# Head features split by parity, weights loaded as whole row pairs, and a reordered prologue in a fused attention and gated-unit kernel

## The chip, the cores and the metric

The kernel runs on one core of a Trainium2 chip. The time is the device time of one execution in microseconds, as the median of several executions; it is 1.6 to 1.9 us above the span, which is the time from the first to the last instruction in the profiled execution. Shorter is better. Every run is marked fast or slow by its clock and its distance from the fastest run of the same kernel. All ratios here are the mean time of one kernel's fast runs over the mean of the other's fast runs of the same rounds, so they are not quite the ratio of the medians that stand beside them. The bracket behind a ratio is its 95% interval. Slower and faster mean below that this interval excludes 1.

## The reference

The first half is causal attention over 8 batches, 12 heads, 448 positions and 64 features per head. The second half takes the heads side by side as 768 features and applies a causal convolution of five taps, a sigmoid gate, and two 768x768 products.

```python
scores = q @ k.T / sqrt(64);  causal mask;  attn = softmax(scores);  x = attn @ v   # (8, 12, 448, 64)
x = x.transpose(0, 2, 1, 3).reshape(8, 448, 768)
gate = sigmoid(sum(conv_w[t] * shift(x, 4 - t) for t in range(5)))
out = (gate * (x @ w_val)) @ w_out
```

## The kernel before

The work is cut into 24 units of four heads of one batch. A unit goes through `scores` in two stages (TensorE into the four banks of `sc_ps`), exponentials on ScalarE, causal masks on GpSimd, `attend` (the denominators into `den_ps`, the values into `av_ps`), `normalize` on VectorE, which writes the tile `x`, then `conv` and the gate. Three units make a batch; `val` multiplies a batch's x by `w_val` and VectorE multiplies in the gate; `project` multiplies a pair of batches by `w_out`. In the timelines each engine works through its instructions in the order in which the program gives them (in the trace before, a gate product whose last matmul ended at 60.85 us began only at 65.00, behind the transposes of unit 8 that the program has ahead of it and that waited for their loads), and the whole schedule is set by hand.

The 64 features of a head are stored as two halves of 32. In partition 32*h+d of the tile `x` stand feature d of head h and, in a second column block, feature 32+d. That is why a weight load is made of many small pieces: feature d and feature 32+d are 32 rows apart in DRAM.

```python
def load_wv(i, j):                          # 12 requests in all
    g, swap = VERSIONS[i]
    nc.gpsimd.dma_start(out=wv_sb[i][32 * j:32 * (j + 1)],
                        in_=w_val.rearrange("(g h e d) f -> g h d e f", h=G, e=2, d=32)[g, j ^ swap])
...
def val(b, g, o):
    for e in range(2):
        ...  # six matmuls into o[e]
        nc.vector.scalar_tensor_tensor(     # gate product, one instruction of 128 partitions
            out=gv[g][:, e, S * (b % 2):S * (b % 2 + 1)], in0=gates[NG * b + g][:, e], scalar=1.0,
            in1=o[e][:, 0:S], op0=ALU.add, op1=ALU.mult)
```

The body of the kernel goes two units at a time. The loads of q and k run some units ahead, v runs three units ahead, and `transposes(n + 1)` puts q and k of the next unit into the form that `scores` needs. `keep_clock` issues matmuls of zeros, fillers, that only keep TensorE busy.

```python
def first_half(n):
    exps(n, 0)                              # scores, exponentials and masks of stage 0
    transposes(n + 1)
    cast_v(n)
    load_v(n + 3)
    for m in {4: (6,), 5: (7,), 6: (8, 9), 7: (10, 11)}.get(n, (n + 4,)):
        load_qk(m)
...
exps(3, 1)                                  # the end of the prologue
cast_v(3)
load_v(6)
transposes(4)
next_val((z_ps, den_ps))
```

The softmax here doesn't subtract the row's maximum and nothing guards it: scores larger than these inputs give would overflow.

## Time and profile before

| what | before |
|---|---|
| time, median of 3 runs | 229.48 us (229.06 to 229.81) |
| profiled span | 227.8 us |
| TensorE busy | 209.1 us, 92% |

Two rows of the page's slices are useful to add: each digit is a fortieth of the span, here 5.7 us, in tenths of busy time (PE) or of the full TensorE clock (PEclk).

```profile
PE   7887789889749999999999999999999999989993
PEclk9999999999979999999999999999999999999999
```

From the thirteenth slice on TensorE is nearly full until the end. Almost all that a schedule can win is in the first twelve, and the lowest digit there, a 4, is the hole near 63 us.

### The profile page before, as it was taken

What the parts mean: (1) busy time and instruction counts of PE and PEld (TensorE: products, weight loads), DVE (VectorE), ACT (ScalarE), POOL (GpSimd) and SP (SyncE); (2) the same over time, 40 slices, a digit from 0 to 9 for tenths busy, and PEclk for the clock granted to TensorE, in tenths of its full rate; (3) what the DMA queues carried; (4) which work ended last, traced back from release to release, by engine and by line L of the source; (5) the groups of instructions that cost most, each with busy time, mean ns of one, the idle gap of its engine ahead of it and who ended that gap; (6) DMA issues with size and microseconds to landing.
All of it is one profiled execution on the core that took longest, in us unless ns stands there. A gap on an engine that the chain in (4) does not pass through costs nothing.

```text
span 227.8 us, 8749 instructions
## 1 busy us (share of the span) xinstructions
PE 209.1 (92%) x3822; PEld 114.2 (50%) x3822; DVE 139.6 (61%) x251; ACT 140.0 (61%) x178; POOL 111.5 (49%) x192
## 2 busy tenths in 40 slices
PE   7887789889749999999999999999999999989993
PEld 3334434445325555455555555555655555546551
DVE  7745877565576871868847947939738656270300
ACT  2388226878435779656777687587877777505142
POOL 7189963874950771855727707727535245100000
PEclk9999999999979999999999999999999999999999
DMA  5999999899999289594892993886855120301334
GB/s 85 181 214 201 210 216 202 163 236 210 205 242 202 52 157 308 125 225 82 162 244 82 230 278 73 159 242 114 167 187 154 43 101 3 138 3 72 140 123 156
DMA packets 57696, 36.37 MB, mean 160 GB/s; under 512 B 46133, under 2 KB 54069, under 8 KB 57658
## 3 DMA queue, kind: packets, MB, share of 16 engines
q1 hardware_dynamic: 48922, 22.44, 36.9%
q0 software_dynamic: 8736, 13.37, 34.2%
q8 instruction: 30, 0.49, 0.9%
q14 instruction: 8, 0.07, 0.1%
HBM read 37.76 MB, written 11.01 MB: 214 GB/s over the span
## 4 chain that ended last, share of the span: by engine, by line
PE 70%; DMA 10%; DVE 6%; SPq 5%; ACT 4%; issue 3%; POOL 1%; DVEq 0%; POOLq 0%; ACTq 0%
PE z_ps L263 11%; PE den_ps L263 11%; PE z_ps L285 10%; PE sc_ps L181 8%; PE av_ps L215 6%; PE sc_ps L241 6%; PE den_ps L285 5%; DMA kb<-in_k_dram 5%; PE den_ps L215 4%; SPq L78 3%; PE av_ps L285 3%; ACT pt L190 3%; DMA vf<-in_v_dram 3%; PE sc_ps L285 2%; DMA wv<-wv 2%
## 5 line engine op out<-in xcount | busy, mean ns | idle before, releaser
L190 ACT ACTIVATE pt<-sc_ps 128x1024 bf16<-128x1024 f32 x96 | 93.0, 1022 | 36.6 <-PE sc_ps L181 35.1
L194 POOL TENSOR_SCALAR_AFFINE_SELECT pt<-pt 128x512 bf16<-128x512 bf16 x24 | 15.7, 653 | 71.3 <-ACT pt L190 71.2
L285 PEld LDWEIGHTS <-gv 128*32 128x32 bf16 (+1 forms) x624 | 31.6, 97 | 21.9 <-issue 4.3
L263 PEld LDWEIGHTS <-wv 128*128 128x128 bf16 x288 | 26.4, 98 | 27.1 <-issue 4.3
L181 PE MATMUL sc_ps<-qt,kt 32*128 32x448 bf16 (+3 forms) x768 | 34.9, 280 | 3.3 <-ACT pt L190 1.7
L285 PE MATMUL z_ps<-wo,gv 128*32 128x384 bf16 (+1 forms) x462 | 33.2, 326 | 0.8 <-DVE gv L266 0.8
L200 POOL TENSOR_SCALAR_AFFINE_SELECT pt<-pt 128x512 bf16<-128x512 bf16 x48 | 30.3, 661 | 7.0 <-ACT pt L190 7.0
L181 PEld LDWEIGHTS <-kt 32*128 32x128 bf16 x768 | 18.3, 94 | 29.0 <-issue 17.8
L263 PE MATMUL den_ps<-x,wv 128*128 128x448 bf16 x138 | 30.5, 354 | 1.1 <-DVE x L228 0.8
L263 PE MATMUL z_ps<-x,wv 128*128 128x448 bf16 x138 | 30.2, 353 | 0.9 <-DVE x L228 0.9
L248 ACT ACTIVATE gate<-sc_ps 128x896 f32<-128x896 f32 x23 | 19.9, 914 | 17.9 <-PE sc_ps L241 17.9
L266 DVE SCALAR_TENSOR_TENSOR gv<-gate,den_ps 128x448 bf16<-128x448 f32 x23 | 14.1, 611 | 25.2 <-PE den_ps L263 25.2
L228 DVE TENSOR_TENSOR x<-av_ps,rb 128x448 bf16<-128x448 f32 x48 | 27.7, 620 | 2.6
L215 PE MATMUL av_ps<-pt,vb 128*32 128x448 bf16 (+3 forms) x768 | 26.0, 279 | 1.4 <-DVE vb L86 1.4
L165 DVE STREAM_TRANSPOSE qt<-qb 128x448 uint32<-128x448 uint32 x24 | 22.8, 951 | 7.3 <-DMA qb<-in_q_dram 6.7
L222 DVE STREAM_TRANSPOSE dt<-den_ps 128x448 f32<-128x448 f32 x24 | 15.4, 644 | 18.1 <-PE den_ps L215 18.1
L165 DVE STREAM_TRANSPOSE kt<-kb 128x448 uint32<-128x448 uint32 x24 | 22.3, 931 | 4.4 <-DMA kb<-in_k_dram 4.4
L290 ACT ACTIVATE ob<-z_ps 128x384 f32<-128x384 f32 x29 | 14.3, 493 | 16.2 <-PE z_ps L285 16.2
L86 POOL CAST vb<-vf 128x1024 bf16<-128x1024 f32 x21 | 21.8, 1038 | 0.0
L215 PEld LDWEIGHTS <-vb 128*32 128x32 bf16 x768 | 16.7, 99 | 7.3 <-DVE vb L86 1.6
L266 DVE SCALAR_TENSOR_TENSOR gv<-gate,z_ps 128x448 bf16<-128x448 f32 x23 | 14.1, 614 | 7.9 <-PE z_ps L263 7.9
L215 PE MATMUL den_ps<-pt,ones 128*32 128x448 bf16 (+3 forms) x384 | 15.5, 281 | 3.3 <-DVE gv L266 3.1
(46 smaller groups left out, 177.0 us busy)
## 6 DMA issues: line engine op xcount, KB each, us to landing
out_dram<-ob SPq DMA_DIRECT2D x27, 384.0 KB, 3.9
vf<-in_v_dram SPq DMA_DIRECT2D x72, 128.0 KB, 5.5
qb<-in_q_dram POOLq DMA_DIRECT2D x24, 224.0 KB, 4.7
kb<-in_k_dram POOLq DMA_DIRECT2D x24, 224.0 KB, 5.8
vf<-in_v_dram SPq DMA_DIRECT2D x24, 64.0 KB, 5.5
wv<-in_moe_w_val_dram POOLq DMA_DIRECT2D x12, 96.0 KB, 4.5
wo<-in_moe_w_out_dram POOLq DMA_DIRECT2D x6, 192.0 KB, 8.8
wv<-wv SPq DMA_DIRECT2D x4, 96.0 KB, 5.2
```

Of the source, the lines that this page charges most:

```text
L86: engine.tensor_copy(out=t, in_=vfs.pop(n))
L165: nc.vector.transpose(out=t.bitcast(U32).rearrange("p (b s) -> p s b", s=T), in_=qks.pop((name, n)).rearrange("p s d -> p (s d)").bitcast( ...
L181: nc.tensor.matmul(out=sc_ps[h // 2][:, h % 2, c0:c0 + nq], lhsT=kt[r, e, k0:k0 + 128], rhs=qt[r, e, q0:S], start=e == 0, stop=e == 1, ski ...
L190: nc.scalar.activation(out=pt[:, 2 * hp:2 * hp + 2, 512 * stage:512 * (stage + 1)], in_=sc_ps[hp], func=AF.Exp, scale=D ** -0.5)
L194: nc.gpsimd.affine_select(out=pt[:, :, 0:128], in_=pt[:, :, 0:128], compare_op=ALU.is_ge, fill=0.0, base=0, pattern=[[0, G], [1, 128]], ch ...
L200: nc.gpsimd.affine_select(out=pt[:, :, c:c + 128], in_=pt[:, :, c:c + 128], compare_op=ALU.is_ge, fill=0.0, base=0, pattern=[[0, G], [1, 1 ...
L215: nc.tensor.matmul(out=o, lhsT=w, rhs=pt[:, h, col:col + nq], start=i == 0, stop=i == 3, skip_group_check=True, tile_position=(0, 32 * i_out))
L228: nc.vector.tensor_tensor(out=x[:, dh, 4:S + 4], in0=av_ps[dh][:, 0:S], in1=r, op=ALU.mult)
L248: nc.scalar.activation(out=gates[n], in_=sc_ps[u][:, :, 0:S], func=AF.Tanh, scale=0.5)
L263: nc.tensor.matmul(out=o[e][:, 0:S], lhsT=wv_sb[version(NG * b + cg)][:, ce, f:f + 128], rhs=xs[(NG * b + cg) % 8][:, ce, 4:S + 4], start= ...
L266: nc.vector.scalar_tensor_tensor(out=gv[g][:, e, S * (b % 2):S * (b % 2 + 1)], in0=gates[NG * b + g][:, e], scalar=1.0, in1=o[e][:, 0:S], ...
L285: nc.tensor.matmul(out=o[w * j:w * (j + 1), 0:384], lhsT=gvs[p][g][:, dh, 128 * m + w * j:128 * m + w * (j + 1)], rhs=wo_sb[c][:, f], star ...
```

## The change

The intent is threefold. First, a head's features are split by parity: even features in one column block, odd ones in the other. Rows 2p and 2p+1 of a weight are neighbours in DRAM, so a group's weights load as whole pairs of rows, in nine requests instead of 18. Columns of v and of `w_val` are then taken with a step of two. Second, with this split the gate of an odd feature comes out of the convolution two heads away from the value that it multiplies, so the odd gate product becomes two instructions of 64 partitions. Third, the prologue is reordered: the fillers between the score stages go, units 0 and 1 are attended earlier, v of unit 1 is cast earlier and v of unit 2 on ScalarE, v of units 3 and 4 is held back by a one-word memset on the loading tile, attend(3) and two projections are moved ahead of unit 4, and the loads of q and k for units 6 to 8 are called one unit earlier. The diff, cut to its core:

```diff
-    def load_wv(i, j):
+    def load_wv(i):
         g, swap = VERSIONS[i]
+        src = w_val.rearrange("(g p e) f -> g p e f", g=NG, e=2)[g]
+        if swap:
+            for j in range(G):
+                nc.gpsimd.dma_start(out=wv_sb[i][32 * j:32 * (j + 1)], in_=src[32 * (j ^ 1):32 * ((j ^ 1) + 1)])
+        else:
+            nc.gpsimd.dma_start(out=wv_sb[i], in_=src)
 ...   (load_wo and the convolution weights likewise; wo_sb becomes three tiles)
-                    w = ones[:, int(ci == 1)] if dh == 2 else vb[:, c, h, 32 * dh:32 * (dh + 1)]
+                    w = ones[:, int(ci == 1)] if dh == 2 else vb[:, c, h, dh:D:2]
 ...
-                        j = 2 * ((i ^ swapped(n)) % 2) + dh
+                        j = i ^ swapped(n) ^ (2 * dh)
 ...   (val: columns f + e:f + 256:2 of w_val; the last `late` of six matmuls may come after the other bank's)
+                    for r, at in ((slice(0, 64), slice(64, 128)), (slice(64, 128), slice(0, 64))) if e else ((slice(0, 128),) * 2,):
+                        nc.vector.scalar_tensor_tensor(
+                            out=gv[g][r, e, S * (b % 2):S * (b % 2 + 1)], in0=gates[NG * b + g][at, e], scalar=1.0,
+                            in1=o[e][r, 0:S], op0=ALU.add, op1=ALU.mult)
 ...
-            for m in {4: (6,), 5: (7,), 6: (8, 9), 7: (10, 11)}.get(n, (n + 4,)):
+            for m in {4: (7,), 5: (8,), 6: (9,), 7: (10, 11)}.get(n, (n + 4,)):
 ...
+    def hold_v(n, engine):
+        engine.memset(v_f[n % V_BUFS][:, 0, 0, 0:1], 0.0)
+        load_v(n)
 ...   (prologue, from the second stage of unit 0 on; three keep_clock(3) are gone)
+    exps(1, 0, 2)
+    load_wv(1)
+    load_wv(2)
+    transposes(2)
+    cast_v(0, nc.vector)
+    cast_v(1, nc.vector)
+    exps(1, 1, 2)
+    load_wv(0)
+    values(0)
+    exps(2, 0, 2)
+    exps(2, 1, 2)
+    cast_v(2, nc.scalar)
+    values(1)
+    hold_v(3, nc.vector)
+    values(2)
+    load_qk(3)
+    for g in range(NG):
+        load_wo(g)
+    load_qk(4)
+    hold_v(4, nc.gpsimd)
+    load_v(5)
 ...   (conv(0,1), val, transposes(3), conv(2), val, exps(3, 0), load_qk(5), val)
+    cast_v(3)
+    exps(3, 1)
+    load_qk(6)
+    load_v(6)
+    next_outs(1, (z_ps,))
+    values(3)
+    transposes(4)
+    next_outs(1, (z_ps,))
```

More of the change, by code (lines that the diff above doesn't have):

```diff
@@ L85, in cast_v @@
         t = v_pool.tile([128, 4, G, D], BF16, name="vb")
-        engine.tensor_copy(out=t, in_=vfs.pop(n))
+        if engine is nc.scalar:
+            nc.scalar.activation(out=t, in_=vfs.pop(n), func=AF.Copy)
+        else:
+            engine.tensor_copy(out=t, in_=vfs.pop(n))
         vbs[n] = t
     wv_sb = [sb.tile([128, 2, DM], BF16, name=f"wv{i}") for i in range(len(VERSIONS))]
-    wo_sb = [sb.tile([128, DM], BF16, name=f"wo{i}") for i in range(NE)]
-    def load_wv(i, j):
+    wo_sb = [sb.tile([128, 2, DM], BF16, name=f"wo{g}") for g in range(NG)]
+    def load_wv(i):
         g, swap = VERSIONS[i]
-        nc.gpsimd.dma_start(out=wv_sb[i][32 * j:32 * (j + 1)],
-                            in_=w_val.rearrange("(g h e d) f -> g h d e f", h=G, e=2, d=32)[g, j ^ swap])
+        src = w_val.rearrange("(g p e) f -> g p e f", g=NG, e=2)[g]
+        if swap:
+            for j in range(G):
+                nc.gpsimd.dma_start(out=wv_sb[i][32 * j:32 * (j + 1)], in_=src[32 * (j ^ 1):32 * ((j ^ 1) + 1)])
+        else:
+            nc.gpsimd.dma_start(out=wv_sb[i], in_=src)
     def swap_wv():
@@ L99, in swap_wv, with load_wo @@
             nc.sync.dma_start(out=wv_sb[3][32 * j:32 * (j + 1)], in_=wv_sb[2][32 * (j ^ 1):32 * ((j ^ 1) + 1)])
-    def load_wo(c):
-        nc.gpsimd.dma_start(out=wo_sb[c], in_=w_out[128 * c:128 * (c + 1)])
+    def load_wo(g):
+        nc.gpsimd.dma_start(out=wo_sb[g], in_=w_out.rearrange("(g p e) f -> g p e f", g=NG, e=2)[g])
     NV = 2 * len(VERSIONS)
@@ L138, in conv_weights @@
             for dh in range(2):
-                src = cwn.rearrange("t (g h e d) -> t g h e d", h=G, e=2, d=32)[:, g, :, dh]
+                src = cwn.rearrange("t (g h d e) -> t g h d e", h=G, e=2, d=32)[:, g, :, :, dh]
                 dst = cwp[:, 2 * i + dh].rearrange("t (h d) -> t h d", d=32)
@@ L192, in softmax_numerators @@
                 in_=sc_ps[hp], func=AF.Exp, scale=D ** -0.5)
-        if stage == 0:
-            nc.gpsimd.affine_select(out=pt[:, :, 0:128], in_=pt[:, :, 0:128], compare_op=ALU.is_ge, fill=0.0,
-                                    base=0, pattern=[[0, G], [1, 128]], channel_multiplier=-1)
-            nc.gpsimd.affine_select(out=pt[:, :, 448:512], in_=pt[:, :, 448:512], compare_op=ALU.is_ge, fill=0.0,
-                                    base=64, pattern=[[0, G], [1, 64]], channel_multiplier=-1)
-        else:
-            for c in (512, 832):
-                nc.gpsimd.affine_select(out=pt[:, :, c:c + 128], in_=pt[:, :, c:c + 128], compare_op=ALU.is_ge,
-                                        fill=0.0, base=0, pattern=[[0, G], [1, 128]], channel_multiplier=-1)
+        for c, base, w in ((0, 0, 128), (448, 64, 64)) if stage == 0 else ((512, 0, 128), (832, 0, 128)):
+            nc.gpsimd.affine_select(out=pt[:, :, c:c + w], in_=pt[:, :, c:c + w], compare_op=ALU.is_ge, fill=0.0,
+                                    base=base, pattern=[[0, G], [1, w]], channel_multiplier=-1)
     def attend(n):
@@ L238, in conv @@
                     for u, n in enumerate(units):
-                        j = 2 * ((i ^ swapped(n)) % 2) + dh
+                        j = i ^ swapped(n) ^ (2 * dh)
                         r = slice(32 * i, 32 * (i + 1))
                         nc.tensor.matmul(
-                            out=banks[u][i // 2][32 * j:32 * (j + 1), 0:S], lhsT=cwd[r, 2 * version(n) + dh, t],
+                            out=banks[u][dh][32 * j:32 * (j + 1), 0:S], lhsT=cwd[r, 2 * version(n) + dh, t],
                             rhs=xs[n % 8][r, dh, t:t + S], start=t == 0, stop=t == KW - 1, skip_group_check=True,
@@ L253, with val @@
     sc_banks = [[t[:, i] for i in range(2)] for t in sc_ps]
-    def val(b, g, o):
+    def val(b, g, o, late=0):
         gv = gvs.setdefault(b // 2, [None] * NG)
@@ L258, in val @@
             gv[g] = gv_pool.tile([128, 2, 2 * S], BF16, name=f"gv{g}")
-        for e in range(2):
-            f = 128 * (2 * g + e)
-            for c in range(NE):
-                cg, ce = divmod(c, 2)
-                nc.tensor.matmul(out=o[e][:, 0:S], lhsT=wv_sb[version(NG * b + cg)][:, ce, f:f + 128],
-                                 rhs=xs[(NG * b + cg) % 8][:, ce, 4:S + 4],
-                                 start=c == 0, stop=c == NE - 1, skip_group_check=True)
-            nc.vector.scalar_tensor_tensor(
-                out=gv[g][:, e, S * (b % 2):S * (b % 2 + 1)], in0=gates[NG * b + g][:, e], scalar=1.0,
-                in1=o[e][:, 0:S], op0=ALU.add, op1=ALU.mult)
+        for cs in (range(NE - late), range(NE - late, NE)):
+            for e in range(2):
+                f = 2 * G * 32 * g
+                for c in cs:
+                    cg, ce = divmod(c, 2)
+                    w = wv_sb[version(NG * b + cg)][:, ce, f + e:f + 256:2]
+                    nc.tensor.matmul(out=o[e][:, 0:S], lhsT=w,
+                                     rhs=xs[(NG * b + cg) % 8][:, ce, 4:S + 4],
+                                     start=c == 0, stop=c == NE - 1, skip_group_check=True)
+                if NE - 1 in cs:
+                    for r, at in ((slice(0, 64), slice(64, 128)), (slice(64, 128), slice(0, 64))) if e else ((slice(0, 128),) * 2,):
+                        nc.vector.scalar_tensor_tensor(
+                            out=gv[g][r, e, S * (b % 2):S * (b % 2 + 1)], in0=gates[NG * b + g][at, e], scalar=1.0,
+                            in1=o[e][r, 0:S], op0=ALU.add, op1=ALU.mult)
     vals = [(b, g) for b in range(B) for g in range(NG)]
@@ L285, in project @@
                 nc.tensor.matmul(out=o[w * j:w * (j + 1), 0:384], lhsT=gvs[p][g][:, dh, 128 * m + w * j:128 * m + w * (j + 1)],
-                                 rhs=wo_sb[c][:, f], start=c == 0, stop=c == NE - 1, skip_group_check=True,
+                                 rhs=wo_sb[g][:, dh, f], start=c == 0, stop=c == NE - 1, skip_group_check=True,
                                  **(dict(tile_position=(0, w * j)) if tiles > 1 else {}))
@@ L297, in project, with next_val @@
             nc.sync.dma_start(out=rows, in_=ob)
-    def next_val(banks):
+    def next_val(banks, late=0):
         if vals:
-            val(*vals.pop(0), banks)
+            val(*vals.pop(0), banks, late)
     def next_outs(count, banks, tiles=1):
@@ L332, in second_half @@
             exps(n, 1)
-    wv_pieces = [(i, j) for i in range(NG) for j in range(G)]
-    def load_wvs(count):
-        for _ in range(count):
-            load_wv(*wv_pieces.pop(0))
+    def hold_v(n, engine):
+        engine.memset(v_f[n % V_BUFS][:, 0, 0, 0:1], 0.0)
+        load_v(n)
     load_qk(0)
@@ L355 @@
     exps(0, 1, 2)
-    keep_clock(3)
-    load_wvs(8)
     exps(1, 0, 2)
-    keep_clock(3)
+    load_wv(1)
+    load_wv(2)
     transposes(2)
     cast_v(0, nc.vector)
-    load_v(3)
+    cast_v(1, nc.vector)
     exps(1, 1, 2)
-    keep_clock(3)
-    load_wvs(4)
+    load_wv(0)
[6 more added lines that the diff above has]
+    values(2)
     load_qk(3)
-    exps(2, 0, 2)
-    values(0)
-    exps(2, 1, 2)
+    for g in range(NG):
+        load_wo(g)
     load_qk(4)
-    for c in range(NE):
-        load_wo(c)
-    load_qk(5)
-    cast_v(1, nc.vector)
-    load_v(4)
-    values(1)
-    cast_v(2, nc.vector)
+    hold_v(4, nc.gpsimd)
     load_v(5)
     conv((0, 1), sc_banks)
-    values(2)
+    next_val((z_ps, den_ps), 2)
     transposes(3)
+    conv((2,), [av_ps])
     next_val((z_ps, den_ps))
     exps(3, 0)
+    load_qk(5)
     next_val((z_ps, den_ps))
-    conv((2,), [av_ps])
+    cast_v(3)
     exps(3, 1)
-    cast_v(3)
+    load_qk(6)
     load_v(6)
+    next_outs(1, (z_ps,))
+    values(3)
     transposes(4)
-    next_val((z_ps, den_ps))
-    plan = {2: (2, 0, 1, 0, 1), 3: (2, 0, 0, 0, 0), 4: (0, 1, 2, 1, 2), 5: (2, 0, 0, 0, 0)}
+    next_outs(1, (z_ps,))
+    plan = {2: (1, 1, 1, 0, 1), 3: (2, 0, 0, 0, 0), 4: (0, 1, 2, 1, 2), 5: (2, 0, 0, 0, 0)}
     vals_in = {2: (), 3: (2, 4), 4: (0,), 5: (2, 4)}
@@ L407 @@
         second_half(n)
-        values(n - 1)
+        if p > 2:
+            values(n - 1)
         gap(1, (z_ps,), 4)
```

## The prediction

> **What bounds the kernel now.** I read the page first (busy shares, slices), then busy time by stretch, then the chain of work that ended last, then the timeline of the first 72 us and of the end. The busy shares and the stretches (columns: stretch, its length, then busy us and instruction counts of PE, PEld, DVE, ACT, POOL, then clock, DMA share, GB/s):
>
> ```profile
> PE 209.1 (92%) x3822; PEld 114.2 (50%) x3822; DVE 139.6 (61%) x251; ACT 140.0 (61%) x178; POOL 111.5 (49%) x192
> ```
> ```profile
> 20.00:30.00 10.00, 6.80 (x208) 3.93 (x197) 8.59 (x17) 3.87 (x5) 10.00 (x18) 1.00 1.16 216
> ...
> 60.00:70.00 10.00, 6.71 (x154) 3.60 (x154) 6.01 (x10) 2.70 (x4) 5.91 (x11) 0.83 1.12 221
> ...
> 100.00:150.00 50.00, 49.88 (x1004) 27.82 (x1006) 35.59 (x59) 36.19 (x46) 25.58 (x43) 1.00 0.76 166
> 150.00:200.00 50.00, 49.87 (x1016) 28.16 (x1012) 30.82 (x53) 35.11 (x45) 21.39 (x34) 1.00 0.44 123
> ```
>
> From 100 to 200 us TensorE is idle 0.25 us in all: nothing but fewer or shorter matmuls can help there. The losses are ahead of it: over 0 to 70 us the seven ten-microsecond stretches sum to 57.2 us of PE, so 12.8 us idle, and of the busy time 9.2 us are the 22 filler matmuls[...]. In those 70 us the DMA share is near or above 1 except around 42 to 48. The costliest hole is at 62.5 to 65.7, in the chain view (start, length, what):
>
> ```profile
> 57.20 0.54 POOL qb L67
> 57.74 6.43 DMA kb<-in_k_dram
> 64.18 0.02 issue
> 64.20 0.04 DVE kt L165
> 64.24 0.76 issue
> 65.00 0.61 DVE gv L266
> 65.66 1.05 PE den_ps L215 x12
> ```
>
> The k tile of unit 8 (a unit is four heads of one batch) was requested at 57.7 and took 6.4 us. VectorE works in order, so the gate product behind that transpose waited, and with it the attend that needs its PSUM bank: 3.1 us in the waits view. The clock granted is then 0.50 in 66 to 68, and the attend took 2.7 us from 65.66 to 68.34, where a steady one takes 1.4 us: 1.3 us more.
>
> [...] The trace has 98 ns for 128 columns, and about the same for 32[...]. [...] clearing 128x256 words and 64x256 words both took 272 ns.
>
> **The change part by part.**
>
> Weights. Parity order makes two rows of w_val contiguous, so 12 requests become 6 and 6 for w_out become 3. At 0.58 and 0.57 us each on the GpSimd queue, nine fewer are 5.2 us of GpSimd, between 14 and 31 us. The bytes stay. [...] Worth on the path: little, perhaps 0.5 us.
>
> Strided weight columns in val and attend. The key weights already have a stride of two:
>
> ```profile
> L263 PEld LDWEIGHTS <-wv 128*128 128x128 bf16 x288 | 26.4, 98 | 27.1 <-issue 4.3
> L181 PEld LDWEIGHTS <-kt 32*128 32x128 bf16 x768 | 18.3, 94 | 29.0 <-issue 17.8
> ```
>
> 94 ns strided against 98 ns plain, under a val matmul's spacing of 190 ns: cost 0.
>
> Odd gates two heads off. The odd product becomes two 64-partition instructions at 0.61 us each, so 24 x 0.61 = 14.6 us more VectorE, 139.6 to about 153 (one cast goes to ACT). In the steady state it delays the denominator transpose by 0.15 to 0.25 us (today 0.42 us idle before it), whose readers have several us: cost 0. At the end it is on the path. TensorE waits there for the second product today, and a transpose stands behind another:
>
> ```profile
> 199.44 0.62 DVE L266 SCALAR_TENSOR_TENSOR gv<-gate,z_ps 128x448 bf16<-128x448 f32 x1 [0.51 <-PE z_ps L263]
> ...
> 199.98 0.64 DVE L222 STREAM_TRANSPOSE dt<-den_ps 128x448 f32<-128x448 f32 x1
> ...
> 205.16 1.16 PE L285 MATMUL z_ps<-wo,gv 128*32 128x384 bf16 x24 [0.78 <-DVE gv L266]
> ```
>
> That is +0.6 before the last unit's x, +0.6 before the projection at 205, and +0.6 before the projection after the last val (216.1): +1.8 us, exposed.
>
> Prologue. Three of the fillers' six groups go, of which the one at 11.9 to 13.35 stood in front of scores(1,0) and left ACT idle 1.03 us. The exponentials of units 0 to 2 (12 x 0.97 us from 8.9) then end near 22.3 instead of 22.7: attend(0) now stands before scores(2,0) and gives most of it back. Then by the durations of the trace: attend(1) 21 to 22.4, its normalize chain 2.9 us to x(1) at 24.4, attend(2)'s values need the av bank so 24.4 to 25.5, x(2) 27.3, conv(0,1) to 26.7, the eight early val matmuls to 28.2, the late four to 29.0. Today the first val ends at 32.0: 3.0 us won. Then conv(2) 1.1 and val 2.3: scores(3,0) at 32.4 (today 32.16, with 3.4 us less done).
>
> Then it loses. After exp(3,0), ending 35.1, GpSimd does its masks 1.1, load_qk(5) 1.1, the cast of v 1.05, and only then the masks of stage 1 (1.25): attend(3) starts at about 39, its normalize ends near 42.3, and transposes(4), behind it on VectorE, takes 1.9: scores(4,0) at 44.2. Today it is at 39.12, with two projections and an attend (3.4 us) still to do. Pair 2 then needs a score stage's round trip of 2.7 us (45.18 to 47.91 today) three times plus 4.5 to the next pair (47.91 to 52.44): 12.6, so scores(6,0) at 56.8 (today 52.44). Pair 3: 2.7 + 2.6 + 2.9 (scores and val) + 2.6 (exponential) + 1.2 (conv) + 2.3 (val) = 14.3, so scores(8,0) at 71.1. Today this pair takes 19.7 us, because it holds two projections (1.9) and the kt hole (4.4). The hole goes: load_qk(8) is called one unit earlier.
>
> Sum: scores(8,0) 71.1 against 72.1, so -1.0; end +1.8; weights -0.5: +0.3, or 229.8 us. I shade this to 227.5. The sum takes every round trip in full, although projections and transfers may overlap better, and the placement of holds and loads looks as if set by measurement; an estimate by 2 us in the favourable direction is the choice I make.
>
> **The rivals.** (a) The prologue tightens as meant and the kt hole was the main thing: of 4.4 us of hole and 3.0 us of early val nothing is given back, so 7.4 - 1.8 gives 223.9. For it: the chain shows the hole plainly. Against: the v cast and the late transposes(4), both in-order queues. (b) A wait takes the place of the hole: transposes(4) behind normalize(3), or the first projection waiting for w_out, now behind fewer but whole requests with landing times of 7.3 to 10.4 us today. Two such waits of 1.5 us more than counted: 232. (c) Without the fillers TensorE stays at the slow clock until about 20 us: the filler matmuls take 0.49 us each at 12 us and 0.27 at 14.2[...]. attend(0) then takes 1.4 us longer, and scores(2,0) and ACT follow: +1 us. (d) Weight bytes, not requests, set the DMA pace and are hidden anyway: then the parity split buys nothing and costs its 1.8 us, 231 with no prologue gain.
>
> **Range and chances.** The worked sum is 229.8 and the best rival 223.9; the middle, weighted to the sum, is 227.5. My errors on each of three landmarks are about 1.5 us, added in squares 2.6, so 80% is about 3.5 to either side, widened a little: 223.5 to 231.5. Faster by 2% needs less than 224.9, nearly all of rival (a): 0.27. Slower by 2% needs more than 234.1, two of the bad rivals together: 0.07. Within 2%: 0.66.
>
> **What would show each step.** Fillers: ACT without a gap between the stages of unit 1, and filler count 13 instead of 22. First val: its last matmul at about 29. The give-back: scores(4,0) near 44, with VectorE's transposes(4) directly behind x(3); if it comes before 41, rival (a) is right. The hole: no wait of over 1 us for kb or kt around 60, and no granted clock of 0.5. Odd product: 72 product instructions of 0.61 us instead of 48, and the wait before the projection near the end at 1.4 us or more. Weights: 98 ns or close to it in val; if 128-column strided loads took over 190 ns, val would stretch and the kernel be slower by 2% or more, which would prove me wrong in the steady state.

The sum came to 229.8 us, 0.3 above the 229.5 of the kernel before, and was shaded to 227.5. What some of its terms rest on: the 0.61 us for a product of 64 partitions on the two clearings that took 272 ns each, with 128 partitions as with 64 (after the change the products of 64 partitions took 0.62 us, those of 128 took 0.61 to 0.62); "about the same for 32" columns on 99 ns for the columns of v; that VectorE works in order on the product at 65.00 us described above. The "about 20 us" of rival (c) and the 0.5 us for the weights are estimates. What the fillers do to the clock is shown only by later runs: from 12 to 18 us it was 1.00 in e10, which has them, and 0.50 in e13, which is e10 without them.

## The result, and the profile after

The changed kernel took 236.08 us (235.36 to 237.52, four runs) against 229.41 us (229.06 to 229.81, four runs) for the kernel before beside it. The ratio is 1.0298 [1.0247, 1.0349]: slower by 3%, outside the predicted range. The profiled spans are 234.5 and 227.8 us.

The page's busy shares and two of its slice rows, after the change:

```profile
PE 214.6 (92%) x3831; PEld 116.7 (50%) x3831; DVE 154.6 (66%) x275; ACT 141.3 (60%) x179; POOL 107.0 (46%) x184
...
PE   7898997587699999999999999999999999969993
...
PEclk9965699769979999999999999999999999999999
```

VectorE has 24 instructions and 15.0 us more than before; about 14 were worked out. GpSimd has eight fewer. The clock is the row to look at: before it dips once, here it dips in three places, and TensorE has a 5 at 41 to 47 us where it had an 8.

The busy time by stretch, for the stretches that the prediction showed and for 40 to 50 us (columns as there):

```profile
20.00:30.00 10.00, 9.91 (x201) 5.96 (x201) 5.30 (x11) 5.33 (x7) 6.33 (x13) 0.64 0.89 158
...
40.00:50.00 10.00, 5.60 (x70) 2.67 (x70) 5.84 (x9) 1.97 (x5) 3.25 (x5) 0.71 1.15 236
60.00:70.00 10.00, 8.21 (x120) 4.38 (x121) 7.00 (x12) 6.71 (x8) 5.84 (x11) 0.83 1.02 220
100.00:150.00 50.00, 49.37 (x1036) 27.66 (x1032) 40.92 (x68) 35.31 (x43) 27.73 (x47) 1.00 0.77 171
150.00:200.00 50.00, 49.95 (x1089) 28.28 (x1078) 37.36 (x63) 36.19 (x47) 23.06 (x37) 1.00 0.48 126
```

In 20 to 30 us TensorE looks full, at 9.91 of 10, but the clock granted was 0.64. A busy engine at a low clock is not a fast one: the two groups of matmuls of attend(1) took 1.05 and 1.91 us here, and 0.62 and 1.05 us in e9, where the clock was 1.00. In 60 to 70 us it is busier than before, 8.21 for 6.71, so the old hole is smaller. The new loss is in 40 to 50 us: TensorE busy for 5.60 at a clock of 0.71, while the DMA share is 1.15. The chain of work that ended last shows what was waited for there (start, length, what):

```profile
24.77 1.15 DVE x L230 x2
...
25.97 0.38 SPq L78
...
27.56 13.00 DMA vf<-in_v_dram
...
40.69 1.04 POOL vb L89
41.72 1.18 POOL pt L202 x2
...
42.94 0.32 PE den_ps L217 x8
...
45.00 1.16 DVE x L230 x2
46.16 0.85 DVE qt L173
47.01 0.77 DVE kt L173
...
47.82 1.04 PE sc_ps L189 x13
```

Read it upward from the bottom. The scores of unit 4 began at 47.82, as soon as the transposes of q and k for unit 4 were done. These stood behind normalize(3) on VectorE. normalize(3) needed attend(3), which needed the masks of unit 3, which stood behind the cast of v on GpSimd. The cast needed the v tile, whose last request took 13.00 us to land. And that load was only issued at 25.97, because the memset of `hold_v` stood behind x of unit 1 on VectorE. SyncE's queue shows that the fourth of v's requests was itself stuck (start, time in issue):

```profile
25.97 1.54 SPq L78 DMA_DIRECT2D vf<-in_v_dram  x3
27.56 6.66 SPq L79 DMA_DIRECT2D vf<-in_v_dram  x1
```

Between 24.3 and 28.0 GpSimd had just issued q and k of unit 3, the whole of w_out, and q and k of unit 4; these were under way beside it. That they are what held it is argued: no run moved them away. Against the chain before, where the waits named q and k of unit 8, the blame has moved from k at 57 us to v at 27 us.

At the end, the timeline answers to the lines shown before:

```profile
204.04 1.25 DVE L273 SCALAR_TENSOR_TENSOR gv<-gate,z_ps 64x448 bf16<-64x448 f32 x2 [0.51 <-PE z_ps L267]
...
205.33 0.65 DVE L224 STREAM_TRANSPOSE dt<-den_ps 128x448 f32<-128x448 f32 x1
...
211.14 1.16 PE L292 MATMUL z_ps<-wo,gv 128*32 128x384 bf16 x24 [1.41 <-DVE gv L273]
```

The odd product is now 1.25 us in two instructions, the transpose waits behind both, and TensorE's wait ahead of the projection grew from 0.78 to 1.41 us.

To follow where the time went, I use the start of the first score matmul of a unit's first stage as a landmark. The differences add up to the span's:

| stretch, in us | before | after | difference |
|---|---|---|---|
| start to scores(3,0) | 32.16 | 34.31 | +2.15 |
| to scores(4,0) | 6.96 | 13.51 | +6.55 |
| to scores(6,0) | 13.32 | 12.63 | -0.69 |
| to scores(8,0) | 19.60 | 15.51 | -4.09 |
| to the end | 155.76 | 158.54 | +2.78 |
| span | 227.8 | 234.5 | +6.7 |

Of the 8.7 us by which scores(4,0) is later (2.15 + 6.55), 3.4 us are work moved ahead: two projections and attend(3). They lie in the second stretch, which gave up about as much TensorE work, conv(2) and one val, to the first. The following stretches give back 4.8 us, the closed hole included.

### The profile page after: what moved, and what is told of

It reads as the page before. It is cut to its first block, busy times and chain, and to the rows that moved or that the text cites. A ratio compares the mean times of both kernels' runs of the same rounds, so it can differ in the third digit from the quotient of the medians.

```text
span 234.5 us, 8777 instructions
## 1 busy us (share of the span) xinstructions
PE 214.6 (92%) x3831; PEld 116.7 (50%) x3831; DVE 154.6 (66%) x275; ACT 141.3 (60%) x179; POOL 107.0 (46%) x184
## 4 chain that ended last, share of the span: by engine, by line
PE 61%; DMA 14%; ACT 9%; DVE 5%; POOL 3%; issue 3%; SPq 2%; POOLq 0%; ACTq 0%; DVEq 0%
DMA vf<-in_v_dram 12%; PE sc_ps L189 11%; PE z_ps L292 8%; ACT pt L198 8%; PE den_ps L267 8%; PE z_ps L267 7%; PE av_ps L217 7%; PE den_ps L292 5%; PE sc_ps L243 5%; PE den_ps L217 4%; PE av_ps L292 3%; SPq L78 2%; PE sc_ps L292 2%; DMA kb<-in_k_dram 2%; POOL vb L89 2%
## 5 line engine op out<-in xcount | busy, mean ns | idle before, releaser
L202 POOL TENSOR_SCALAR_AFFINE_SELECT pt<-pt 128x512 bf16<-128x512 bf16 x96 | 55.0, 601 | 89.1 <-ACT pt L198 89.0
L189 PE MATMUL sc_ps<-qt,kt 32*128 32x64 bf16 (+3 forms) x768 | 37.9, 290 | 7.5 <-ACT pt L198 5.5
L292 PE MATMUL z_ps<-wo,gv 128*32 128x384 bf16 (+1 forms) x486 | 35.3, 329 | 1.4 <-DVE gv L273 1.4
L189 PEld LDWEIGHTS <-kt 32*128 32x128 bf16 x768 | 19.6, 96 | 34.1 <-issue 22.7
L273 DVE SCALAR_TENSOR_TENSOR gv<-gate,z_ps 64x448 bf16<-64x448 f32 (+1 forms) x43 | 26.6, 620 | 8.6 <-PE z_ps L267 8.0
L273 DVE SCALAR_TENSOR_TENSOR gv<-gate,den_ps 128x448 bf16<-128x448 f32 (+1 forms) x26 | 16.0, 615 | 20.0 <-PE den_ps L267 19.8
L217 PE MATMUL av_ps<-pt,vb 128*32 128x448 bf16 (+3 forms) x768 | 28.1, 293 | 0.0
L217 PEld LDWEIGHTS <-vb 128*32 128x32 bf16 x768 | 17.7, 103 | 6.7 <-issue 1.4
L217 PE MATMUL den_ps<-pt,ones 128*32 128x448 bf16 (+3 forms) x384 | 16.5, 293 | 3.7 <-POOL pt L202 3.5
L292 PE MATMUL den_ps<-wo,gv 128*128 128x384 bf16 x84 | 17.0, 342 | 0.0
```

What stands on the lines that cost most here:

```text
L189: nc.tensor.matmul(out=sc_ps[h // 2][:, h % 2, c0:c0 + nq], lhsT=kt[r, e, k0:k0 + 128], rhs=qt[r, e, q0:S], start=e == 0, stop=e == 1, ski ...
L202: nc.gpsimd.affine_select(out=pt[:, :, c:c + w], in_=pt[:, :, c:c + w], compare_op=ALU.is_ge, fill=0.0, base=base, pattern=[[0, G], [1, w] ...
L217: nc.tensor.matmul(out=o, lhsT=w, rhs=pt[:, h, col:col + nq], start=i == 0, stop=i == 3, skip_group_check=True, tile_position=(0, 32 * i_out))
L273: nc.vector.scalar_tensor_tensor(out=gv[g][r, e, S * (b % 2):S * (b % 2 + 1)], in0=gates[NG * b + g][at, e], scalar=1.0, in1=o[e][r, 0:S], ...
L292: nc.tensor.matmul(out=o[w * j:w * (j + 1), 0:384], lhsT=gvs[p][g][:, dh, 128 * m + w * j:128 * m + w * (j + 1)], rhs=wo_sb[g][:, dh, f], ...
```

## The experiments

My theory after the result: the late v of unit 3 and the transposes behind normalize(3) cost the prologue what the closed hole had won, and the split product costs some 3 us behind it. The rivals were: the new layout with its larger requests starves the loads; the missing fillers leave a slow clock, which sets the prologue; the earlier q and k loads gain nothing. Fifteen experiments ran. All were correct. The profiles of e3 and e14 fell in the slow state, so no landmark of theirs stands in the table. Each row is one execution. That of before took 229.68 us, and in the later sessions its fast runs averaged 227.8 to 228.3, so a landmark of a later kernel set against this row can look better by 1 to 2 us than the times do. The landmarks of the others:

| kernel | scores(3,0) | scores(4,0) | scores(6,0) | scores(8,0) | (8,0) to end |
|---|---|---|---|---|---|
| before | 32.16 | 39.12 | 52.44 | 72.04 | 155.8 |
| e1 layout only | 31.40 | 38.37 | 51.58 | 70.01 | 159.1 |
| e4 before, q and k early | 32.04 | 38.99 | 51.63 | 66.22 | 156.2 |
| e12 e4 and casts early | 32.38 | 39.34 | 51.78 | 66.37 | 155.9 |
| e15 e12, one filler group less | 31.85 | 38.80 | 51.24 | 65.83 | 155.5 |
| after | 34.31 | 47.82 | 60.45 | 75.96 | 158.5 |
| e9 after again | 32.55 | 47.15 | 59.37 | 74.80 | 158.8 |
| e2 schedule only | 34.32 | 46.35 | 58.90 | 73.48 | 155.6 |
| e5 fillers back | 32.04 | 47.44 | 59.66 | 74.26 | 159.3 |
| e6 v of unit 3 early | 33.03 | 45.06 | 57.62 | 72.21 | 158.8 |
| e7 w_out in single rows | 34.01 | 47.90 | 60.52 | 75.94 | 158.7 |
| e8 transposes first | 38.55 | 47.86 | 60.09 | 74.68 | 158.7 |
| e10 three repairs | 33.42 | 42.75 | 54.97 | 69.56 | 158.6 |
| e11 e10, old layout | 35.57 | 46.11 | 58.68 | 73.27 | 156.2 |
| e13 e10 without fillers | 33.17 | 42.50 | 54.72 | 69.31 | 158.8 |

### Layout or schedule: e1, e2, e3

**e1** is the kernel before with the parity layout, the nine requests and the split product, in the old order.

```diff
-    load_wvs(8)          # and the 32-feature halves, one product per bank
+    load_wv(0)
+    load_wv(1)
...
-    load_wvs(4)
+    load_wv(2)
```

> The schedule of before with the parity layout, nine weight requests and the split odd product. Theory schedule (the prologue's order and holds lose the first 4 to 5 us, the layout only the 2 to 3 us of the split product): 231.4 to 232.5 us, scores(8,0) within 0.7 us of the 72.0 of before, the end from scores(22,0) about 2.1 us longer. Theory layout (large weight requests starve the v loads, or the strided weights slow the prologue): 234 to 236, with scores(8,0) at 75 or later.

Measured: 232.69 us (230.75 to 235.11), ratio 1.0175 [1.0103, 1.0246], slower, by less or more than 2%. Its prologue is no worse than before; its landmark scores(8,0) is even 2.0 us earlier, in part because the clock stayed full there (1.00 from 60 to 70 us, where before had 0.83). All of the loss lies behind it: 159.1 us instead of 155.8.

**e2** is the opposite: the new order of work with the old layout, 18 requests and one product per bank.

```diff
-    load_wv(1)
-    load_wv(2)
+    for j in range(G):
+        load_wv(1, j)
+    for j in range(G):
+        load_wv(2, j)
...
-                    for r, at in (...) if e else (...):      # two products of 64 partitions
+                    nc.vector.scalar_tensor_tensor(          # one of 128
```

> The schedule of after with the layout, the 18 weight requests and the single odd product of before. Theory schedule: 233 to 234.5 us, with scores(4,0) still near 47 and scores(8,0) near 75. Theory layout: 229 to 231, with the v load of unit 3 landing in under 8 us (13.5 in after) and scores(4,0) near 44.

Measured: 233.03 us (230.86 to 233.51), ratio 1.0229 [1.0176, 1.0283], slower. The prologue is as late as in the changed kernel to within 1.5 us at scores(4,0), and the end is as short as before. So the two faults are separate: the order of work costs the prologue, the layout costs the end. In this one trace v of unit 3 had landed when its cast started, at 39.18, and the transposes of unit 4 behind normalize(3) were the wait that remained. That the smaller requests had let v through earlier is possible; one trace does not show it.

**e3** is the kernel before with nothing but the odd product split.

```diff
-            nc.vector.scalar_tensor_tensor(
-                out=gv[g][:, e, ...], in0=gates[NG * b + g][:, e], ...)
+            for r in (slice(0, 64), slice(64, 128)) if e else (slice(0, 128),):
+                nc.vector.scalar_tensor_tensor(
+                    out=gv[g][r, e, ...], in0=gates[NG * b + g][r, e], ...)
```

> The kernel before with nothing changed but the odd product in two 64-partition halves: 24 more VectorE instructions. If the split costs only where it stands on the path, at the end: +1.8 to +2.8 us, 231.2 to 232.2, the end from scores(22,0) longer by 2.1. If it is hidden everywhere: 229.4. If VectorE at about 66 per cent also delays the steady state: over 233.

Measured: 231.3 us over four runs, of which two were slow; the two fast ones took 228.78 and 229.53 us, ratio 1.0048 [0.9978, 1.0117]. That is inconclusive for the time: it allows no cost, and not quite the 1.0127 that 2.9 us would be. What the split costs is better read from the landmarks of all other runs. From scores(8,0) to the end, the six kernels with one odd product per val (before, e2, e4, e11, e12, e15) need 155.5 to 156.2 us, and the nine with the split (after, e1, e5 to e10, e13) 158.5 to 159.3, with no overlap, whatever their order of work. The mean difference is 2.9 us. About 2.0 us of it are behind scores(22,0): 46.18 us before, 48.20 after, and 48.20 to 48.21 in all nine. The other 0.8 us lie between scores(8,0) and scores(14,0): 46.0 us on average without the split, 46.8 with it. Since e1 changes the whole layout and e3's profile was slow, what is shown is the cost of the layout; that the product is its carrier is shown at the end, where TensorE's waits name it (1.4 and 0.5 us for `gv` after, 0.8 before), and only argued for the 0.8 us. The slow profile of e3, which changes nothing but the product, agrees with both: 48.19 us behind scores(22,0), and 46.61 between scores(8,0) and scores(14,0).

### What the closed hole is worth: e4

**e4** is the kernel before with q and k of units 6 to 8 requested one unit earlier, and nothing else.

```diff
-            for m in {4: (6,), 5: (7,), 6: (8, 9), 7: (10, 11)}.get(n, (n + 4,)):
+            for m in {4: (7,), 5: (8,), 6: (9,), 7: (10, 11)}.get(n, (n + 4,)):
...
     cast_v(3)
+    load_qk(6)
     load_v(6)
```

> The kernel before with q and k of units 6, 7 and 8 requested one unit earlier, as after does. If the hole at 62.5 to 65.7 comes from the late request of kt(8): it closes, 3 to 4.4 us less, 225 to 226.5 us. If the DMA engines are full and the transfer arrives at the same time anyhow: 229 to 230, with the hole still there or moved to a v load.

Measured: 224.3 us (223.58 to 224.75) against 227.94 in the same session, ratio 0.9832 [0.9785, 0.9879]. This is better than both kernels. In its page the clock never dips, and in its timeline the transpose of k for unit 8 starts without a wait for its load, followed by the attend:

```profile
PEclk9999999999999999999999999999999999999999
```
```profile
57.53 1.42 PE L263 MATMUL den_ps<-x,wv 128*128 128x448 bf16 x6
...
59.26 0.92 DVE L165 STREAM_TRANSPOSE kt<-kb 128x448 uint32<-128x448 uint32 x1
...
60.70 0.62 PE L215 MATMUL den_ps<-pt,ones 128*32 128x448 bf16 x16
```

That transpose was at 64.20 before, and scores(8,0) is 5.8 us earlier than in the one trace of before. By the mean times of the same session the gain is 3.8 us, 224.2 against 228.0. So this piece of the third part of the change brings its own gain; in the changed kernel the rest took it back.

### Which part of the new order costs: e9, e5, e6, e8, e7

**e9** is the changed kernel once more, for a second trace and more runs beside the others.

```diff
(no edit)
```

> The kernel after, unchanged, so that it stands beside the repaired ones on one chip. 234 to 236.5 us, ratio to before 1.025 to 1.035; every theory expects this.

Measured: 236.06 us (234.51 to 237.62, six runs), ratio 1.0345 [1.0289, 1.0401]. The time repeats; the trace shows what varies. scores(3,0) came at 32.55, 1.8 us earlier than in the first trace, and yet scores(4,0) came at 47.15, only 0.7 earlier, because the cast of v started at 40.01 after waiting 2.58 us for its load; in the first trace it started at 40.69 after 1.51. The load's landing sets scores(4,0), not the work ahead of it.

**e5** puts the three filler groups back.

```diff
     exps(0, 1, 2)
+    keep_clock(3)
     exps(1, 0, 2)
+    keep_clock(3)
...
     exps(1, 1, 2)
+    keep_clock(3)
```

> The kernel after with the three groups of three filler matmuls back. Theory clock (the half clock from 13 to 27 us comes from the missing fillers and is on the path): no granted 0.5 before 27 us, scores(3,0) at 32 to 33 instead of 34.3, but scores(4,0) still waits for the v load of unit 3, so the total moves by 0 to 1 us only. Rival (fillers cost more than the clock gives): scores(3,0) at 34 or later and a total of 236 to 237.

Measured: 234.86 us (234.09 to 237.56), ratio 1.032 [1.0228, 1.0412], as slow as e9 within the intervals. scores(3,0) came at 32.04, and the gain was lost at once to the same wait, now longer:

```profile
40.19 1.04 POOL L89 CAST vb<-vf 128x1024 bf16<-128x1024 f32 x1 [3.28 <-DMA vf<-in_v_dram]
```

**e6** takes the hold off v of unit 3 and loads it where the kernel before did, behind the cast of unit 0.

```diff
     cast_v(0, nc.vector)
+    load_v(3)
     cast_v(1, nc.vector)
...
-    hold_v(3, nc.vector)
```

> The kernel after with the v load of unit 3 issued right after the cast of unit 0, as before does, instead of held until x(1). Theory hold: it lands by 25 us, attend(3) starts at 39 to 40 instead of 42.4, scores(4,0) at 44 to 45 instead of 47.8, the total 2 to 4 us less, 232 to 234. Rival (the weights and k tile then arrive later[...]): first val or transposes(4) wait instead, total 235 to 237.

Measured: 233.1 us (232.77 to 234.6), ratio 1.0243 [1.0179, 1.0306]. Its timeline shows the cast 2.8 us earlier and without a wait, and then the next thing in line:

```profile
37.89 1.07 POOL L89 CAST vb<-vf 128x1024 bf16<-128x1024 f32 x1
...
45.06 0.63 PE L189 MATMUL sc_ps<-qt,kt 32*128 32x448 bf16 x16 [2.63 <-DVE kt L173]
```

TensorE now waits 2.63 us for the transposes that stand behind normalize(3). scores(4,0) is at 45.06 instead of 47.82: two waits stood one behind the other, and taking away the first uncovers the second.

**e8** takes away the second alone.

```diff
-    values(3)
     transposes(4)
+    values(3)
```

> The kernel after with transposes(4) ahead of values(3) on VectorE. Prediction's step (transposes(4) behind normalize(3) delays scores(4,0)): scores(4,0) at about 44.5 to 45, behind attend(3) and the projection only; total 1.5 to 3 us less. Rival (the k tile of unit 4 lands so late that it gains nothing): scores(4,0) at 47 or later, total 236.

Measured: 234.62 us (232.88 to 235.52), ratio 1.0278 [1.0214, 1.0343]. The time says little. In the trace the stretch from scores(3,0) to scores(4,0) shrank from 13.5 to 9.3 us, but the stretch ahead of it grew, for a reason of its own: v of unit 2 landed so late that its cast on ScalarE waited 3.81 us, to 26.71. Why it did so in this execution is open.

**e7** loads w_out as six requests whose pieces are single rows instead of three with pairs.

```diff
-        nc.gpsimd.dma_start(out=wo_sb[g], in_=w_out.rearrange(...)[g])
+        for e in range(2):
+            nc.gpsimd.dma_start(out=wo_sb[g][:, e], in_=w_out.rearrange(...)[g, :, e])
```

> The kernel after with w_out in six requests of single rows (3 KB runs) instead of three of row pairs (6 KB runs); same bytes, same place. Theory packet size[...]: the v load of unit 3 lands 2 us or more earlier than the 13.5 us of after, scores(4,0) earlier by as much. Rival (bytes, not run length): landing within 1 us of after, total 235.5 to 237.

Measured: 236.99 us (235.36 to 237.84), ratio 1.0383 [1.0318, 1.0448], and the cast of v waited 1.88 us, to 40.76. The wait stands as it was, so the form of the w_out requests is not what makes v late.

### The repairs together: e10, e11, e13, e14

**e10** joins e5, e6 and e8.

```diff
+    keep_clock(3)        # three times, as in e5
+    load_v(3)            # behind cast_v(0), as in e6; hold_v(3) removed
-    values(3)
     transposes(4)
+    values(3)
```

> The kernel after with the three prologue repairs together: fillers back, v of unit 3 not held, transposes(4) ahead of values(3). Theory (these three are the prologue's loss, each hidden by the others alone): scores(4,0) at 41 to 43, scores(8,0) at 68 to 70 against 76.0 in after, total 228 to 230 us. Rival (something else, such as DMA order or GpSimd, binds next): scores(8,0) at 72 or later, total 232 or more.

Measured: 231.65 us (229.66 to 234.66), ratio 1.0139 [1.0075, 1.0202]. Its timeline, for the lines that were late:

```profile
38.28 1.06 POOL L89 CAST vb<-vf 128x1024 bf16<-128x1024 f32 x1
38.85 0.91 DVE L173 STREAM_TRANSPOSE kt<-kb 128x448 uint32<-128x448 uint32 x1
...
42.75 0.63 PE L189 MATMUL sc_ps<-qt,kt 32*128 32x448 bf16 x16
```

The transposes run at 38 to 40 us, in VectorE's idle time, and scores(4,0) starts with no wait on record at 42.75, 5.1 us earlier than in the changed kernel. scores(8,0) is at 69.56, 2.5 us ahead of the kernel before. What keeps it slower is the end, 158.6 us.

**e13** is e10 without the fillers, for the rival of the slow clock.

```diff
-    keep_clock(3)        # the three that e10 added
```

> The kernel after with v of unit 3 not held and transposes(4) ahead of values(3), but without the fillers. Theory (the half clock between 12 and 27 us is on the path): 1 to 2 us slower than e10, ratio to before 1.018 to 1.023, granted 0.5 in several stretches before 27 us. Rival (the clock is hidden behind the DMA and the casts): ratio as e10, 1.012 to 1.016.

Measured: 231.44 us (229.79 to 235.3), ratio 1.0161 [1.009, 1.0232]. The clock in its profile was 0.50 from 12 to 18 us, where e10 had 1.00, and the landmarks and the time are those of e10 to within 0.3 us. A half clock of this length cost nothing measurable. That fits ScalarE's exponentials and the loads setting the pace there, which no run shows by itself. It does not speak for the first trace of the changed kernel, where the half clock lasted until 26 us (see the fillers below).

**e14** is e10 without the swap of the transposes, that is e5 and e6.

```diff
-    transposes(4)
     values(3)
+    transposes(4)
```

> The kernel after with the fillers and v of unit 3 not held, but transposes(4) still behind values(3). Theory (VectorE's order costs about the 2.6 us that scores(4,0) waits for kt in e6): ratio 1.02 to 1.027, scores(4,0) at 44 to 45.5 against 42.75 in e10. Rival: ratio as e10, the wait being made up by scores(8,0).

Measured: 234.96 us (233.05 to 237.74), ratio 1.0292 [1.021, 1.0375] over the fast runs. Against e10 the order of the transposes is worth about 1.5%, some 3.5 us, once v is early. Its profile was slow, with v of unit 2 late again, so a part of this may belong to that. The traces give a cleaner figure: from scores(3,0) to scores(4,0) it takes 12.02 us in e2 and e6, where v had landed and the transposes stood behind normalize(3), and 9.32 to 9.33 in e8, e10 and e13, where they stood ahead of it: 2.7 us.

**e11** is e10 with the old layout and one odd product.

```diff
(e10, with the layout lines of the kernel before, as in e2)
```

> The same three repairs with the layout, the 18 requests and the single odd product of before. Theory (the split product costs 2.9 us after scores(8,0) and nothing ahead of it): 2.5 to 3.2 us less than e10, 225 to 227 us, from scores(8,0) to the end 155.5 to 156.3 us. Rival (nine requests win as much in the prologue): within 1 us of e10.

Measured: 231.38 us (228.54 to 233.81), ratio 1.0074 [1.0005, 1.0143]. Its end is 2.4 us shorter than e10's, as the theory wants, but the time gained is less than that and the intervals overlap. In its trace the prologue was longer: scores(3,0) at 35.57, with the cast of v of unit 2 waiting 1.80 us for its load. The twelve and six requests in this order may do that; it is open.

### A version that beats both: e12, e15

**e12** is e4 with the casts of v taken from the change.

```diff
     load_v(3)
+    cast_v(1, nc.vector)
...
     load_qk(5)
-    cast_v(1, nc.vector)
+    cast_v(2, nc.scalar)
     load_v(4)
     values(1)
-    cast_v(2, nc.vector)
```

> The kernel before with q and k one unit earlier (e4) and with v of unit 1 cast right behind unit 0 on VectorE and unit 2 on ScalarE, as after does. If attend(1)'s wait for its cast was on the path: scores(3,0) 0.5 to 1.5 us earlier than e4 and the total 222.5 to 224 us. If the DMA or the GpSimd masks bind there anyway: 224 to 225, as e4.

Measured: 223.96 us (223.2 to 224.82), ratio 0.9813 [0.9772, 0.9855]. That is the best ratio, but its interval covers e4's, and scores(3,0) did not come earlier: the early casts add nothing that can be measured.

**e15** takes one group of fillers out of e12, the one that the prediction said kept ScalarE idle.

```diff
     exps(0, 1, 2)
-    keep_clock(3)
     load_wvs(8)
```

> e12 without the filler group ahead of scores(1,0). If that group is on the path, as the prediction says: ScalarE has no gap before exp(1,0), 0.3 to 1 us less than e12, 223 to 223.8. If the group is needed for the clock: granted 0.5 appears between 12 and 24 us and the time is 225 or more.

Measured: 223.72 us (223.07 to 224.86), ratio 0.9839 [0.9795, 0.9883]. Its timeline shows that the step itself works: ScalarE runs six exponentials without a gap.

```profile
8.38 5.64 ACT L193 ACTIVATE pt<-sc_ps 128x1024 bf16<-128x1024 f32 x6 [6.29 <-PE sc_ps L184]
```

In the one trace of each, every landmark from scores(3,0) on is about 0.5 us earlier than in e12, as expected if the gap of 1 us that this group of fillers made is partly on the path. The times, 0.3 us apart in the mean and from two sessions, neither show this nor rule it out.

## Why the prediction was wrong

The worked sum was 229.8 us, the number 227.5, the measurement 236.08. The 6.3 us between sum and measurement divide by the sum's own terms: scores(8,0) came 4.9 us late, the part behind it cost 1.0 us more than worked out, and the 0.5 us credited to the weights did not show. Another 2.3 us are the shade.

**The step that failed** is "attend(3) starts at about 39 ... scores(4,0) at 44.2". It counted GpSimd's instructions up to the cast of v, and took the tile as landed by then. The trace has the cast at 40.69 and scores(4,0) at 47.82. Of these 3.6 us, 1.9 are scores(3,0) coming at 34.31 instead of 32.4, most of it with a half clock (see the fillers below), and 1.5 are the cast's wait for the load. In the second trace scores(3,0) was on time, at 32.55, and the wait took 2.58. Either way the load fixes the time. Where v had landed (e2, e6), scores(3,0) to scores(4,0) took 12.02 us, against 11.8 in the sum, so nothing else in this step was wrong by much. The chain of the kernel before names v loads only up to 21.6 us and none for unit 3, whose load was issued behind the cast of unit 0; the diff says where the new one is issued, and I did not follow it into the queue. I had noted a DMA share of 1.1 to 1.2 from 10 to 40 us (1.12, 1.16 and 1.16 by stretches of ten) and thought, without a figure, of what early v loads do to the rest; I did not turn the thought round and ask what the rest does to v. (In e10, with v of unit 3 early, scores(3,0) came at 33.42 us, in e5 at 32.04; this is one trace each and shows no cause.) Without the hold (e6) scores(4,0) came 2.8 us before the first trace and 2.1 before the second; counted from scores(3,0), which moved too, it is 1.5 and 2.6 us.

**The transposes behind normalize(3)** were foreseen and right in kind. The 2.63 us in e6, and the 2.7 us between the traces with one order and the other, confirm them. Rival (b) named both this wait and w_out as waits that take the hole's place; it was given 232 us and stood outside the middle of my range. It was the true story, with v in the place of w_out.

**From scores(4,0) on** the working was good: 12.6 us to scores(6,0) predicted, 12.63 measured; 14.3 to scores(8,0) predicted, 15.51 measured. Nearly 0.9 of this last difference goes with the clock. In all profiled runs with early q and k whose clock stayed full from 60 to 70 us this stretch is 14.58 to 14.60 us; in the three where it fell (after, e7, e9; 0.50, 0.57 and 0.50 in its lowest stretch of 2 us) it is 15.42 to 15.51. That is a cost of the clock at 64 to 68 us, a place that rival (c) did not name.

**The hole** closed as predicted. I took 4.4 us for it; e4 has 5.8 us at scores(8,0) between single traces and 3.8 us between mean times, so the size was about right.

**The split product** was worth +1.8 at the end by the prediction; the landmarks say 2.0. "In the steady state ... cost 0" was wrong by the 0.8 us between scores(8,0) and scores(14,0). Behind it the rule held: from scores(14,0) to scores(22,0) both kernels need 63.55 us.

**The weights.** The strided columns cost nothing, as predicted. In val the group's line has the same 98 ns as before (in attend it is 103 against 99 ns, in a trace with more time at the half clock):

```profile
L267 PEld LDWEIGHTS <-wv 128*128 128x128 bf16 x288 | 26.7, 98 | 26.5 <-issue 3.9
```

Nine requests instead of 18 took 5.0 us of GpSimd's queue instead of 10.0, and this saved nothing that can be measured on the path.

**The fillers and the first val.** By my steps the first val ends at 29.0 and scores(3,0) follows at 32.4. In the second trace they were at 29.0 and 32.55; in the first, where the clock was 0.50 from 14 to 26 us, at 30.8 and 34.31. In the second the clock was back by 20 us. Here is attend(1), first trace and then second:

```profile
21.96 1.05 PE L217 MATMUL den_ps<-pt,ones 128*32 128x448 bf16 x16
22.81 1.91 PE L217 MATMUL av_ps<-pt,vb 128*32 128x448 bf16 x32
```
```profile
21.31 0.62 PE L217 MATMUL den_ps<-pt,ones 128*32 128x448 bf16 x16
21.75 1.05 PE L217 MATMUL av_ps<-pt,vb 128*32 128x448 bf16 x32
```

From the second score stage of unit 2 to the first convolution TensorE took 7.1 us in the first trace, without a wait on record, and 5.6 in the second, with waits: 1.5 us that go with the clock. e2 and e7, where the clock was 0.66 both from 10 to 20 and from 20 to 30 us (0.67 and 0.64 in the first trace), have scores(3,0) at 34.32 and 34.01. So rival (c), which gave the missing fillers +1 us, was right in kind for these executions, and wrong for the second. It did not decide scores(4,0), which is only 0.7 us apart in the two traces, because v's load did. Why the clock came back at 20 us in one execution and at 27 in another is open. Nor is a long wait on record before it was lost: in the first trace it fell at about 13.5 us, worked out from 0.87 on average from 12 to 14 and 0.50 after, with no wait of TensorE on record longer than 0.62 us since 9.6. And the 1.00 that the views show before that is not to be relied on: at 8.2 us three fillers took 0.49 us each there, at 14.2 us in the kernel before 0.27.

**The shade** was a poor choice, though not what put the result outside: around the unshaded 229.8 a range of the same width would have ended at 233.8. I had a worked sum with named round trips, and moved it by 2.3 us on the thought that such a change had probably been tuned. Nothing in the profile said so. The chance of 0.07 for slower was too small by the same thought: I had counted the bad rivals as independent, while a late load and a late transpose lie in one chain and add up.

What stays open: which of the requests under way beside it made v of unit 3 late, since only their form was tested (e7, e2) and not their place, why v of unit 2 lands late in some executions (e8, e14, e11), how much of the run-to-run spread of the changed kernel this is, and by which wait the split product costs 0.8 us in the middle.

## What to carry to other kernels

When a change moves a load, follow it as a request: when its queue issues it (here the four of v between 25.97 and 27.56 us, the last one landing 13.00 us later), what other queues have issued just before (here q, k and w_out between 24.3 and 28.0; that these held it was not tested), and what stands behind its consumer on the same engine (here the masks of unit 3, at 41.67, behind the cast at 40.69); a tile is not there because its program line comes early enough. Test each part of a bundled change alone, for here one part of the bundle, requesting q and k one unit earlier, was worth 1.7% by itself and the rest turned it into a loss of 3%. And keep the worked sum: if the working says 229.8, an adjustment needs a line of the profile behind it.
